# Loads cut into pieces of 256 to 320 KB, and SyncE waits before each transfer for the landing of the one issued four places ahead

## Chip, cores, metric

The kernel runs on one core of one Trainium2 chip, which has eight cores. The metric is the device time of one execution in microseconds (us). Before the change it is 707.77 us, the median of 3 runs (707.77 to 709.53).

## What is computed

One block of a network over 2048 positions with 640 channels, float32 throughout. A small vector `c` gives six rows of modulation (`w_mod` is 640 x 3840). A long convolution along the positions, gated by `q`, is followed by a two-layer perceptron of width 1728 with a squared ReLU.

```python
mod = (_silu(c) @ w_mod).reshape(1, 6, 1, -1)          # sa, ca, ga, sb, cb, gb
h = _layernorm(x) * (1 + ca) + sa                       # x = A_q, 2048 x 640
# _A_ref: a causal convolution of k with 4 taps, times v, then per channel a
# convolution with ssm_k over all 2048 positions (by rfft of length 4096),
# plus kv * ssm_D, times its first argument
x = x + ga * _A_ref(h, A_k, A_v, A_shift_k, A_ssm_k, A_ssm_D)
h = _layernorm(x) * (1 + cb) + sb
r = relu(h @ w1 + b1)
x = x + gb * ((r * r) @ w2 + b2)                        # w1 640 x 1728, w2 1728 x 640
```

## The kernel before

**Stages.** The channels are worked in five blocks b = 0 to 4 of 128. For each block K and V are loaded (`kv_load`, four quarters of 512 positions), transposed on TensorE (`kv_k`, `kv_v`), convolved and multiplied on VectorE (`kv_s`, `kv_m`), and stored to a scratch tensor `kv_d` in HBM in the same quarters (`kv_m`, 256 KB each). `load_x` reads them back in another layout: 128 partitions, each with 32 groups of 64 numbers, 1 MB a block. `load_h` reads the filter `ssm_k` in that layout, also 1 MB. The convolution is a Fourier transform made of matmuls. Its first step is `unit_a` (line 368, tile `pa`), which takes a quarter of a block at a time from the filter (i = 1) or from the data (i = 0). Then come `spectrum` (line 383, tiles `eh`, `h` and `x`; constants `gb`), the complex product on VectorE and GpSimd (`front`), the inverse steps `back` (line 449, tile `qp`, constants `gi`) and `unit_t`, `unit_y` (lines 513, 524). `skip` adds `ssm_D` to the filter; for b above 0 VectorE does it.

**Beside it.** The layer norm of `q` loads all of `q` in tiles of one to four rows of 128 positions (`q_big`, `q_ut`, both through `q_load`) and takes statistics on VectorE (`stats1`, line 284). For each block `q` is loaded again as a column strip of 1 MB (`load_xp`), scaled on ScalarE (`prep_a`) and gated. The sum goes to a second scratch tensor, `x1_d` (`finish_add`). The modulation rows come from `w_mod` in slabs of 320 KB (`part_load`), scaled on ScalarE (line 326) and added on GpSimd.

**The perceptron** starts at about 305 us: eight chunks of 256 positions, in each 14 steps over the width (lines 707 and 777). Its weights are loaded in slabs of 320 KB (`w_load`) into four staging buffers and split in two parts.

**Order.** The program is written as one list. A table (`at`, with the places `FS` and `GS`) puts each load and each piece of side work at a place among the TensorE steps, and `keep_order` at the end ties every engine to the order in which the program was written. Almost all transfers go through `sp_dma` (line 138), that is from SyncE (SP), which issues them one after the other: a transfer whose data or buffer isn't ready keeps all later ones waiting. A few small constants and two last pieces of the result are issued from ScalarE, two single rows from GpSimd.

**Sizes before.** `load_x(0)` and `load_x(1)` are cut into four pieces of 256 KB, the other `load_x` and all `load_h` after block 0 are single transfers of 1 MB (block 0's filter is loaded in four pieces by `load_h0`). `load_xp` is 1 MB, `q_load` 320 to 1280 KB, `load_gb` and `load_gi` 512 KB, four of each. Everything else is 320 KB or less, except `load_x1` with 640 KB in the perceptron.

**The one wait placed by hand** is `HOLD`: after `load_x(0)` and after `load_x(1)` the next transfer waits until the third of the four pieces has landed.

Of the kernel before, what the change touches and what calls it, by code (L numbers as in the profile page):

```python
# [18 lines left out]
P = 128  # L19
NB = D // P  # L20
NL = S // P
# [4 lines left out]
NC = S // CH  # L26
EPS = 1e-5
MLAG = 3
HOLD = {0: 2, 1: 2}


def _constants():
# [60 lines left out]
def ssm_mlp_kernel(  # L93
# [20 lines left out]
    nc = tc.nc  # L114
# [16 lines left out]
    kv_d = dr.tile([D, S], F32, tag="kv_d", name="kv_d")  # L131
    x1_d = dr.tile([S, D], F32, tag="x1_d", name="x1_d")

    behind = []


    def sp_dma(o, i):
        sp.dma_start(o, i)
        if behind:
            info = mybir.DependencyInfo(mybir.DependencyClass.Sync, mybir.DependencyReason.DATA)  # L140
            tc.add_manual_dep(nc.cur_bb.bb.instructions[-1], behind.pop(), info, reason="place in time")

    def copy(eng, o, i):
        if eng is act:
# [55 lines left out]
    def p_tile(b):  # L200
        pt[b] = sb.tile([P, 2, DG, 64], F32, tag=f"S{b % 2}", name=f"p_{b}")

    def load_h(b, n=1):
        w = DG // n
        for i in range(n):
            sp_dma(
                pt[b][:, 1, i * w : (i + 1) * w],
                hsrc[:, b * DG + i * w : b * DG + (i + 1) * w, :],
            )

    def load_x(b, n=1):
        w = DG // n
        for i in range(n):
            sp_dma(
                pt[b][:, 0, i * w : (i + 1) * w],
                xsrc[:, b * DG + i * w : b * DG + (i + 1) * w, :],
            )
            if i == HOLD.get(b):
                held = nc.cur_bb.bb.instructions[-1].name
        if b in HOLD:  # L220
            behind.append(held)


    def kv_load(i):
        b, h = divmod(i, 4)
        rows = slice(h * 512, (h + 1) * 512)
        cols = slice(b * P, (b + 1) * P)
        t = KN[h % (4 if b == 0 else 2)]
        for w, src in ((0, k), (1, v)):
            sp_dma(t[:, w], src[rows, cols].rearrange("(t p) d -> p t d", p=P))  # L230
# [128 lines left out]
    def unit_a(b, i, q):  # L359
        t = [  # L360
            ps.tile([P, 8, 32, 2], F32, tag="X", name=f"pa_{b}_{i}_{q}_{e}", bufs=4)
            for e in range(2)
        ]
        for g in range(8):
            for e in range(2):
                l = slice(64 * e, 64 * e + 64)
                for r in range(2):
                    pe.matmul(  # L368
                        t[e][64 * r : 64 * r + 64, g].rearrange("p m d -> p (m d)"),
                        pt[b][l, i, 8 * q + g, :],  # L370
                        cw[l, r],
                        start=True,
                        stop=True,
                    )
        for e in range(2):
            c = 64 * e + 16 * q
            o = AX[b][i][:, :, c : c + 16].rearrange("p m (g d) -> p m g d", d=2)
            copy(act, o, t[e].rearrange("p g m d -> p m g d"))
# [90 lines left out]

    def load_xp(b):  # L470
        t = sb.tile([P, NL, P], F32, tag=f"XP{b % 2}", name=f"xp_{b}")
        sp_dma(t, q[:, b * P : (b + 1) * P].rearrange("(l p) d -> p l d", p=P))
        XPt[b] = t

    def u_tile(b):
# [356 lines left out]
    def kv_all(h):  # L832
        kv_k(0, h)
        kv_s(0, h)
        kv_v(0, h, "T")
        kv_m(0, h)
# [11 lines left out]
    kv_all(2)  # L848
    unit_a(0, 1, 2)
    kv_all(3)  # L850
    load_x(0, 4)
    unit_a(0, 1, 3)
    load_gb(3)
    kv_load(4)
    load_gi(0)
    kv_load(5)
    load_gi(1)
    load_h(1)
    load_gi(2)
    load_gi(3)  # L860
# [10 lines left out]
    def FS(b, j):  # L871
        return 28 * b + j

    def GS(b, s):
        return 28 * b + 10 + s

    def at(i, fn, *args):
        tab[i].append((fn, args))
# [17 lines left out]
    for j in range(2):  # L896
# [5 lines left out]
        [GS(0, i) for i in (0, 1, 1, 2)],  # L902
        [GS(0, i) for i in (3, 4, 4, 5)],
    ], "TTYX")
    at(GS(0, 6), load_x, 1, 4)
    at(FS(1, 8), load_x, 2)
    at(GS(1, 16), load_x, 3)
    at(GS(2, 16), load_x, 4)
    at(FS(0, 2), p_tile, 2)
    at(GS(0, 14), load_h, 2)  # L910
    put_kv(2, [
        [GS(0, i) for i in (8, 9, 10, 11)],
# [4 lines left out]
    for b in (3, 4):  # L917
        at(GS(b - 2, 0), p_tile, b)
        put_kv(b, [[GS(b - 2, 4 * h + i) for i in range(4)] for h in range(4)])
        at(FS(2, 0) if b == 3 else GS(2, 1), load_h, b)  # L920


    def q_big(tag, l0):
        n = 4 if tag.startswith("XP") else 3 if tag == "UP1" else 2
        t = sb.tile([P, n, D], F32, tag=tag, name=f"q_{l0}", bufs=2 if tag == "X1" else None)
        q_load(t, l0, n)

    def q_load(t, l0, n):
        sp_dma(t, q[l0 * P : (l0 + n) * P, :].rearrange("(l p) d -> p l d", p=P))
        for i in range(n):  # L930
            qt[l0 + i] = t[:, i]

    def q_ut():
        q_load(UT.rearrange("p l d -> p (l d)")[:, 0:D].rearrange("p (l d) -> p l d", l=1), 15, 1)
# [8 lines left out]
    each(q_do, stats1, [(l,) for l in range(NL)])  # L943
    at(GS(1, 15), stats1_end)
    at(FS(1, 8), load_xp, 0)
    at(FS(2, 1), load_xp, 1)


# [45 lines left out]
    put4(finish_add, 0, [GS(2, s) for s in (3, 4, 5)], (1, 2, 3))  # L994
    put4(finish_stats, 0, [GS(2, s) for s in (5, 6, 7)], (1, 2, 3))
    at(GS(2, 8), load_xp, 2)
    put_u(1, [GS(2, s) for s in (5, 8, 11, 14)])
    put4(gate, 1, [FS(3, s) for s in (0, 1, 2, 3)])
# [221 lines left out]
    for i in range(len(seq) + MLAG):  # L1220
        if i >= MLAG:
            n, f = seq[i - MLAG]
# [7 lines left out]
        if i <= last:  # L1230
            n, f = seq[i]
# [42 lines left out]
```

## Time and profile before

| | |
|---|---|
| median of 3 runs | 707.77 us (707.77 to 709.53) |
| the profiled execution, its own time | 712.27 us |
| its span, first to last instruction | 710.5 us |
| mean granted TensorE clock | 0.989 |
| TensorE (matmul) busy | 666.4 us, 94% |
| VectorE, ScalarE, GpSimd busy | 47%, 47%, 42% |
| DMA: read from HBM, written | 58.98 MB, 14.42 MB |

How to read it: times are microseconds from the first instruction unless marked ns. PE is TensorE's matmuls and PEld its weight loads, which overlap; DVE is VectorE, ACT ScalarE, POOL GpSimd, SP SyncE. L368 is line 368 of the kernel. A "q" after an engine's name means its sequencer, which waits, branches and issues transfers. A row of the timeline reads: start, duration, engine, line, operation, output and inputs by the program's tile names, number of instructions merged, and in brackets the idle time before them with what ended it. "issue" there is time in which the engine waited for nothing that the profile shows. PEclk is the TensorE clock granted, as a share of full speed. In the DMA view q1 is SyncE's queue, q10 ScalarE's, and q8, of kind "instruction", carries packets of 16 KB; a row of issues gives KB each and the microseconds from issue to landing.

### The profile page before, as it was taken

The numbers are of one execution on the slowest core, as the hardware profiler recorded it, in microseconds if no ns is written. First come the engines' busy times: TensorE is split into PE (matmuls) and PEld (weight loads), VectorE is DVE, ScalarE is ACT, GpSimd is POOL, SyncE is SP. The second block draws the span as 40 slices with busy tenths as digits, with TensorE's granted clock in tenths as the row PEclk, the third lists the DMA queues.
The fourth block names the chain that finished last, engine by engine and source line by source line (L and its number), as shares of the span: only waits on it lengthen the run. The fifth ranks groups of instructions, "written<-read, shape, count | busy, mean of one in ns | idle before, by whom it ended". The sixth has DMA issues, their size and how long they took to land.

```text
span 710.5 us, 21027 instructions
## 1 busy us (share of the span) xinstructions
PE 666.4 (94%) x9164; PEld 636.5 (90%) x9164; DVE 336.3 (47%) x661; ACT 330.6 (47%) x685; POOL 295.1 (42%) x338
## 2 busy tenths in 40 slices
PE   6698889879899989999999999999999999999997
PEld 5687778769789879889999999999999999999996
DVE  5284745746877599669831222222313313312313
ACT  4535546666883886557533323323333333233221
POOL 1050036137845978942532522422514415325213
PEclk9999999999999999999999999999999999999999
DMA  9787795869465374328320020020020100200101
GB/s 251 211 248 253 213 259 169 240 192 256 107 186 138 91 195 151 88 88 238 98 75 1 1 75 1 1 75 2 10 66 1 39 37 1 75 1 1 39 1 38
DMA packets 88721, 74.76 MB, mean 105 GB/s; under 512 B 19250, under 2 KB 73906, under 8 KB 88628
## 3 DMA queue, kind: packets, MB, share of 16 engines
q1 hardware_dynamic: 86672, 72.86, 36.1%
q8 instruction: 72, 1.18, 0.7%
q10 hardware_dynamic: 1892, 0.54, 0.3%
q14 instruction: 21, 0.17, 0.1%
q0 software_dynamic: 64, 0.01, 0.0%
HBM read 58.98 MB, written 14.42 MB: 103 GB/s over the span
## 4 chain that ended last, share of the span: by engine, by line
PE 81%; DVE 8%; ACT 5%; issue 3%; DMA 2%; POOL 1%; DVEq 0%; POOLq 0%; SPq 0%; ACTq 0%
PE acc L777 26%; PE h L707 25%; PE qp L449 5%; PE x L383 4%; PE h L383 4%; PE y L524 4%; PE pa L368 4%; DVE KV L253 2%; PE t L513 2%; PE h L698 1%; PE xtp L672 1%; ACT a L145 1%; DVE kacc L253 1%; ACT q L145 1%; ACT KV L482 1%
## 5 line engine op out<-in xcount | busy, mean ns | idle before, releaser
L150 POOL TENSOR_TENSOR mtmp<-mtmp 128x256 f32<-128x256 f32 x112 | 72.1, 644 | 242.3 <-ACT mtmp L739 234.4
L707 PE MATMUL h<-xt,w_S 128*128 128x256 f32 x1290 | 167.0, 281 | 0.1
L707 PEld LDWEIGHTS h<-xt,w_S 128*128 128x128 f32 x1290 | 161.2, 190 | 0.4 <-DVE w_S L156 0.4
L777 PE MATMUL acc<-w_S,hring 128*128 128x320 f32 x960 | 156.8, 311 | 0.2 <-DVE hring L156 0.2
L156 DVE TENSOR_TENSOR hring<-mtmp,hring 128x256 fp32r<-128x256 f32 x112 | 64.9, 580 | 189.9 <-ACT hring L145 189.8
L777 PEld LDWEIGHTS acc<-w_S,hring 128*128 128x128 f32 x960 | 141.8, 188 | 0.7 <-DVE hring L156 0.7
L739 ACT ACTIVATE mtmp<-h,b1t 128x256 f32<-128x256 f32 x104 | 49.4, 475 | 177.6 <-PE h L707 172.2
L145 ACT ACTIVATE hring<-mtmp 128x256 fp32r<-128x256 f32 x112 | 46.7, 417 | 46.2 <-POOL mtmp L150 44.6
L368 PEld LDWEIGHTS pa<-wx,p 64*64 64x64 f32 x2560 | 44.7, 140 | 20.7 <-issue 12.1
L368 PE MATMUL pa<-wx,p 64*64 64x64 f32 x2560 | 51.1, 228 | 12.6 <-issue 3.9
L145 ACT ACTIVATE a<-pa 128x512 f32<-128x512 f32 x80 | 43.5, 599 | 26.7 <-PE pa L368 26.3
L524 PE MATMUL y<-wx,wx 128*64 128x64 f32 x1280 | 46.7, 227 | 8.5 <-ACT wx L145 5.5
L524 PEld LDWEIGHTS y<-wx,wx 128*64 128x64 f32 x1280 | 41.3, 139 | 13.3 <-ACT wx L145 6.2
L150 DVE TENSOR_TENSOR wx<-x,wx 128x512 f32<-128x512 f32 x64 | 40.9, 681 | 25.2 <-PE x L383 15.8
L156 POOL TENSOR_TENSOR we<-wx 128x256 f32<-128x256 f32 x20 | 15.9, 795 | 77.8 <-DVE wx L150 75.6
L674 DVE TENSOR_SCALAR we<-xtp,cbs 128x256 f32<-128x256 f32 x35 | 19.0, 544 | 51.8 <-PE xtp L672 51.8
L153 POOL TENSOR_TENSOR wm<-wm,wm 128x640 f32<-128x640 f32 x20 | 31.8, 1589 | 28.3 <-ACT wm L326 28.1
L383 PE MATMUL x<-a,gb 128*64 128x128 f32 x640 | 41.9, 274 | 1.2 <-ACT a L145 1.1
L253 DVE SCALAR_TENSOR_TENSOR KV<-kt,tap,KV 128x511 f32<-128x511 f32 (+2 forms) x48 | 35.5, 739 | 15.3 <-ACT ktail L145 13.3
L145 ACT ACTIVATE q<-qp 128x512 f32<-128x512 f32 (+1 forms) x40 | 21.3, 584 | 38.5 <-PE qp L449 38.5
L383 PEld LDWEIGHTS x<-a,gb 128*64 128x64 f32 x640 | 36.2, 137 | 2.3 <-ACT a L145 1.3
L383 PE MATMUL h<-a,gb 128*64 128x128 f32 x512 | 35.0, 280 | 0.0
(140 smaller groups left out, 1031.2 us busy)
## 6 DMA issues: line engine op xcount, KB each, us to landing
wm<-in_w_mod_dram SPq DMA_DIRECT2D x25, 320.0 KB, 5.3
KV<-in_A_k_dram SPq DMA_DIRECT2D x20, 256.0 KB, 5.8
KV<-in_A_v_dram SPq DMA_DIRECT2D x20, 256.0 KB, 4.6
xp<-in_A_q_dram SPq DMA_DIRECT2D x5, 1024.0 KB, 9.2
out_dram<-x SPq DMA_DIRECT2D x14, 320.0 KB, 2.8
w1s<-in_B_w_dram SPq DMA_DIRECT2D x13, 320.0 KB, 3.9
w2s<-in_B_w_dram SPq DMA_DIRECT2D x13, 320.0 KB, 3.9
kv_d<-KV SPq DMA_DIRECT2D x16, 256.0 KB, 4.2
```

The costliest lines, as they stand in the source:

```text
L145: act.activation(o, i, AF.Copy)
L150: eng.tensor_mul(o, a, b)
L153: eng.tensor_add(o, a, b)
L156: eng.tensor_sub(o, a, b)
L253: dve.scalar_tensor_tensor(o, x, tap[:, b, t : t + 1], o, op0=ALU.mult, op1=ALU.add)
L368: pe.matmul(t[e][64 * r : 64 * r + 64, g].rearrange("p m d -> p (m d)"), pt[b][l, i, 8 * q + g, :], cw[l, r], start=True, stop=True,)
L383: pe.matmul(t[64 * a : 64 * a + 64, s + r], gb[:, g, r, a], AX[b][i][:, 2 * g + a], start=True, stop=True,)
L449: pe.matmul(t[a][:, u], gi[l, 4 * j + u, r], w[r][l, u % 2], start=(r == 0), stop=(r == 1),)
L524: pe.matmul(y[64 * h : 64 * h + 64, 4 * (g % 2) + i].rearrange("p c l d -> p (c l d)"), tss[g][:, i, 64 * r : 64 * r + 64], ca[:, r, h], s ...
L707: pe.matmul(hps[n, f][:m], WI[1, f][:, a, b], XT[n][:, x, b], start=(b == 0 and i == 0), stop=(b == NB - 1 and i == 2),)
L739: act.activation(r[:m], h[:m], AF.Relu, bias=b1t[:m, f : f + 1])
L777: pe.matmul(acc[2 * s + i], h[:, a, s * P : (s + 1) * P], w[:, y, i * 320 : (i + 1) * 320], start=(f == 0 and ti == 0), stop=(f == NF - 1 ...
```

## The change

`sp_dma` remembers the name of every transfer that it issues. From the fifth on, each is given a dependency on the one four places ahead of it (`OUT = 4`): SyncE waits for that one's landing before it issues. `HOLD` and its two waits are gone. `load_h` and `load_x` always issue four pieces of 256 KB, `load_xp` four of 256 KB, `q_load` one piece of 320 KB for each row of 128 positions. `load_gb`, `load_gi` (512 KB) and `load_x1` (640 KB) keep their sizes. No arithmetic and no order changes.

```diff
-HOLD = {0: 2, 1: 2}
+OUT = 4
...
-    behind = []
+    queued = []
 
     def sp_dma(o, i):
         sp.dma_start(o, i)
-        if behind:
+        queued.append(nc.cur_bb.bb.instructions[-1].name)
+        if len(queued) > OUT:
             info = mybir.DependencyInfo(mybir.DependencyClass.Sync, mybir.DependencyReason.DATA)
-            tc.add_manual_dep(nc.cur_bb.bb.instructions[-1], behind.pop(), info, reason="place in time")
+            tc.add_manual_dep(nc.cur_bb.bb.instructions[-1], queued[-1 - OUT], info, reason="place in time")
...
-    def load_h(b, n=1):
+    def load_h(b, n=4):
...
-    def load_x(b, n=1):
+    def load_x(b, n=4):
...
-            if i == HOLD.get(b):
-                held = nc.cur_bb.bb.instructions[-1].name
-        if b in HOLD:
-            behind.append(held)
...
     def load_xp(b):
...
-        sp_dma(t, q[:, b * P : (b + 1) * P].rearrange("(l p) d -> p l d", p=P))
+        src = q[:, b * P : (b + 1) * P].rearrange("(l p) d -> p l d", p=P)
+        for l in range(0, NL, 4):
+            sp_dma(t[:, l : l + 4], src[:, l : l + 4])
...
-    load_x(0, 4)
+    load_x(0)
...
-    at(GS(0, 6), load_x, 1, 4)
+    at(GS(0, 6), load_x, 1)
...
     def q_load(t, l0, n):
-        sp_dma(t, q[l0 * P : (l0 + n) * P, :].rearrange("(l p) d -> p l d", p=P))
         for i in range(n):
+            sp_dma(t[:, i], q[(l0 + i) * P : (l0 + i + 1) * P, :])
             qt[l0 + i] = t[:, i]
```

## The prediction, made before the changed kernel ran

> **What bounds the kernel now.** First the page, then busy time by stretch.
>
> ```profile
> span 710.5 us, 21027 instructions
> PE 666.4 (94%) x9164; PEld 636.5 (90%) x9164; DVE 336.3 (47%) x661; ACT 330.6 (47%) x685; POOL 295.1 (42%) x338
> PE 81%; DVE 8%; ACT 5%; issue 3%; DMA 2%; POOL 1%; DVEq 0%; POOLq 0%; SPq 0%; ACTq 0%
> ...
> 0.00:305.00 305.00, 266.49 (x6121) 238.64 (x6122) 200.31 (x400) 185.03 (x367) 149.79 (x162) 0.98 0.70 192
> 305.00:710.50 405.50, 399.91 (x3044) 397.88 (x3042) 136.03 (x262) 145.54 (x318) 145.28 (x176) 1.00 0.13 40
> ```
>
> After 305 us PE is busy 399.91 of 405.50 us and the DMA engines 13%: nothing to win there by transfers. Before 305 us PE stands idle 38.5 us and DMA is busy 70%. The rest of this text is about that front part. Of the chain that ended last, 16% (DVE 8, ACT 5, DMA 2, POOL 1) isn't PE's: 114 us, nearly all in the front, so there about 37% ends on others and 63% on PE, its issue time included.
>
> Next, the idle places of PE whose releaser is "issue", from the timeline:
>
> ```profile
> 32.43 0.75 PE L368 MATMUL pa<-wx,p 64*64 64x64 f32 x37 [0.84 <-issue]
> 56.73 0.59 PE L449 MATMUL qp<-wx,gi 64*128 64x128 f32 x3 [1.48 <-issue]
> 91.16 1.13 PE L368 MATMUL pa<-wx,p 64*64 64x64 f32 x33 [2.89 <-issue]
> 135.96 0.60 PE L241 MATMUL kt<-ident,KV 128*128 128x128 f32 x4 [1.81 <-issue]
> 251.14 0.80 PE L524 MATMUL y<-wx,wx 128*64 128x64 f32 x20 [1.66 <-issue]
> ```
>
> PE waits there for no tile. What it waits for, the table of DMA queues shows: q8, kind "instruction", 1.18 MB in 72 packets, so 16 KB each.
>
> ```profile
> q8 instruction: 72, 1.18, 0.7%
> ```
>
> I took the times at which they begin and counted PE's instructions between them (matmuls and weight loads, the third and fourth figure of a row):
>
> ```profile
> 379.78:396.41 16.63, 16.63 (x130) 16.63 (x129) 4.34 (x8) 6.92 (x15) 5.29 (x8) 1.00 0.01 1
> 80.52:83.90 3.38, 2.98 (x129) 2.47 (x130) 3.31 (x9) 1.73 (x5) 0.00 (x0) 1.00 0.78 156
> 80.52:88.72 8.20, 5.65 (x227) 4.64 (x226) 8.02 (x21) 3.91 (x9) 0.00 (x0) 1.00 0.87 245
> 215.52:222.40 6.88, 6.88 (x126) 6.71 (x124) 5.79 (x9) 2.00 (x4) 4.54 (x7) 1.00 0.95 224
> 215.52:224.95 9.43, 9.43 (x170) 9.14 (x168) 8.31 (x13) 3.68 (x7) 5.41 (x8) 1.00 0.93 245
> ```
>
> With DMA at 1% a packet follows the last after 259 instructions. That is PE's code, fetched block by block. After the packet at 80.52 the next was due, by that count, at 83.90; it began at 88.72, 4.8 us late and 453 instructions on, and PE stood still until 91.16. In the stretch 83.9 to 88.6 the queue table has the first row below and no q8; the second is from 88.7 to 88.8:
>
> ```profile
> q1 hardware_dynamic: 1205, 1.43, 92.9%
> ...
> q8 instruction: 1, 0.02, 58.8%
> ```
>
> So a code block waits while SyncE's queue moves 1.43 MB. The counter-example is in the last two rows above: due at about 222.5, begun at 224.95, so 2.4 us late. Then the queue held four transfers of 320 KB (the DMA view from 215.3 to 221.5), the depth that the change allows everywhere:
>
> ```profile
> wm<-in_w_mod_dram SPq DMA_DIRECT2D x4, 320.0 KB, 5.7
> ```
>
> How deep the queue is now:
>
> ```profile
> SPq L138 <- DMA tap<-in_A_shift_k_dram: 1.3, 1, 1.3
> ...
> 35.97 10.78 SPq L138 DMA_DIRECT2D gi<-in_gi_dram  x2
> 88.65 9.70 SPq L138 DMA_DIRECT2D KV<-in_A_k_dram  x1
> ```
>
> SP waits for `tap`, which ScalarE issued and none of SP's transfers needs; it is the ninth transfer that does so, so eight may be out today, of up to 1280 KB. Around 36 and 89 us SP even sat 10 us in an issue.
>
> Last, the clock:
>
> ```profile
> 57.00:59.90 2.90, 2.90 (x31) 2.90 (x31) 0.00 (x0) 0.00 (x0) 0.00 (x0) 0.50 1.11 369
> 89.00:91.00 2.00, 0.00 (x0) 0.00 (x0) 0.00 (x0) 0.00 (x0) 0.00 (x0) 0.92 1.01 345
> 91.20:94.00 2.80, 2.80 (x53) 2.68 (x54) 0.00 (x0) 1.08 (x2) 0.00 (x0) 0.50 1.09 322
> ...
> 56.73 3.58 PE qp L449 x24
> 40.77 1.99 PE qp L449 x32
> ```
>
> Two of the stalls are followed by half clock (0.50); the `qp` block behind the first took 3.58 us instead of 1.99.
>
> **The change part by part.**
>
> *More issues.* 46 more transfers (12 for `load_h`, 9 for `load_x`, 15 for `load_xp`, 10 for `q_load`), each a median of 0.416 us of SP:
>
> ```profile
> L138 SPq DMA_DIRECT2D wm<-in_w_mod_dram x25: 328/416/4481, 71.2 to 241.8; - x25
> ```
>
> 19 us in all, inside the stretches where SP now stands in an issue (10.78 and 9.70 us above) or waits for data. On the path: 0. Without that cover each would make the next load 0.42 us late.
>
> *The window.* Behind a waiting SP stand all later loads: K and V (PE's transposes wait for them), `gi` and `gb` (PE), filters (`skip` on DVE), slabs (ACT), and stores whose buffers are reused. Does it starve them?
>
> ```profile
> 24.16 3.21 DMA p<-kv_d
> 27.51 1.16 PE pa L368 x64
> 28.71 1.16 PE pa L368 x64
> ...
> wm<-in_w_mod_dram SPq DMA_DIRECT2D x1, 320.0 KB, 3.0
> ```
>
> Into idle rings a 256 KB piece lands in 3.21 us, a 320 KB slab in 3.0 (issued at 81.8). Pieces that PE is waiting for come 1.2 us apart (27.51, 28.71). Four pieces are 4.8 us of work against 3.2 to get the next one: the rings don't run dry, and each load lands when it does now, since it stands in one queue either way, only its issue comes later. I take 0. Bounds: 1 us of gain where a filter piece lands sooner, 3.7 of loss (worked out under the rivals).
>
> The Trainium skill, page "DMA: Bandwidth & Descriptors", section "Bandwidth", says the contrary of this change: batch transfers to 1 MiB or more; its section "Anatomy of one DMA — SWDGE (gpsimd) path" gives about 2.0 us fixed for each. By it the sum would gain 46 x 2.0 = 92 us of queue time (an estimate from that page). The trace disagrees for pieces in flight together: 1.2 us apart, fixed part included.
>
> *HOLD gone.* The constants behind `load_x(0)` now wait for its first piece, 27.4 instead of 29.80:
>
> ```profile
> 29.80 0.35 SPq L138 DMA_DIRECT2D gb<-in_gb_dram  x1
> ...
> 49.94 2.06 PE L449 MATMUL qp<-we,gi 64*128 64x128 f32 x32 [0.23 <-DMA gi<-in_gi_dram]
> ```
>
> Gain at most the 0.23 us that PE waits for `gi`; loss at most 2.4 (two pieces of `p` overtaken, 1.2 each), of which the code stall of 0.84 at 32.43 would hide its own length. They stand ahead in the same queue, so 0.
>
> *Code.* With four transfers out a fetch is 2.4 us late instead of 4.8: at 91.16 the stall shrinks by 2.4 to 0.5 us. At 56.73 I take all of 1.48, at 135.96 1.25 of 1.81 (half a microsecond before it PE was waiting for ScalarE in any case). At 251.14 a 1 MB strip alone is out, now and then: 0. At 32.43: 0. Sum 2.4 + 1.48 + 1.25 = 5.1, between 0 (packets wait as now) and 8.7 (all five rows in full).
>
> *Clock.* The idle times left before these places are 1.5 and 1.7 us:
>
> ```profile
> 54.08 1.16 PE L368 MATMUL pa<-wx,p 64*64 64x64 f32 x64 [1.50 <-DVE p L153]
> 87.70 0.57 PE L368 MATMUL pa<-wx,p 64*64 64x64 f32 x23 [1.70 <-DVE KV L270]
> ```
>
> The 1.81 us at 135.96 left the clock whole, so I take both half-clock stretches as gone: 3.58 - 1.99 = 1.6, and half of the 2.8 us from 91.2 = 1.4. Sum 3.0, between 0 and 3.0.
>
> *Together* 8.1 us of PE time in the front. What is late next is VectorE and ScalarE; with 63% of the chain on PE, 5.1 us arrive. Against the profiled execution's own 712.27 us (span 710.5) that is 707.2; the median of the runs shown is 4.5 us lower, so 707.77 - 5.1 = 702.7.
>
> **The rivals.**
>
> *Code doesn't wait for depth.* If a fetch is held up by traffic as such, shallower queues change nothing: 707.8, within 1.5. For it: `gb` and `gi` keep 512 KB, so around 30 to 50 us four transfers can still be 1.5 MB, as much as the 1.43 MB above; the wait then isn't what the change says it shortens. Against it: 4.8 late with deep queues, 2.4 with four slabs. The Trainium skill, same page, section "Queues, rings and completion order", has each DMA engine take turns between queues packet by packet; by that rule a fetch never waits for 1.43 MB of another queue, and this rival holds. The trace disagrees at 83.9 to 88.7.
>
> *More comes through.* If DVE and ACT merely follow PE, and all five stalls go: 8.7 + 3.0 = 11.7 off at most, 8 to 11.7: about 698.
>
> *Slower: four are too few.* Place: the bursts of 30 to 60 and 82 to 109 us.
>
> ```profile
> DMA packets 22154, 15.14 MB, mean 252 GB/s; under 512 B 10240, under 2 KB 19691, under 8 KB 22146
> ...
> KV<-in_A_v_dram SPq DMA_DIRECT2D x20, 256.0 KB, 4.6
> ```
>
> The first 60 us move 252 GB/s. If the 4.6 us median from issue to landing of a V quarter isn't queueing but the transfer's own, four out give 4 x 262 KB / 4.6 us = 228 GB/s, and 57 us of burst become 10.5% longer: 6 us, of which 63%, 3.8, reach the end; PE then idles at 56 and 91 us anyway, so those gains go, and the 1.25 at 136 x 0.63 = 0.8 stays: 710.8. It decides from 4.2 us per landing (4 x 262 / 252). For it: the median lies above that, and PE has only 0.23 us to spare for `gi`. Against it: 3.0 and 3.21 us into idle rings.
>
> **How the numbers follow.** Forecast 0.48, no change 0.19, more 0.10, slower 0.23. About 0.3%, 2.1 us, is what a measurement of this kernel can tell from no change. The forecast's own range is 699.5 to 705.6; with the slower case and part of the larger gain the range is 698 to 711. Faster: 0.48 + 0.10 = 0.58; the same 0.19; slower 0.23.
>
> **What would show it.** PE's "issue" rows at 56, 91 and 136 us gone or under 0.6; no 0.50 clock near 57 and 92 (those at other places stay); a q8 packet never more than about 3 us behind its 256 instructions; no SP issue of 10 us; `gi` and K, V landing within a microsecond of now, so that PE's waits for them don't grow. Wrong would be: "issue" rows as before; or new PE waits named DMA on `kt`, `qp` or `pa`; or the same stalls moved to other places by a code block that falls elsewhere.

## The result, and the profile after

The changed kernel takes 710.51 us, the median of 20 runs (707.17 to 714.6); the kernel before, in 20 runs beside them, 707.09 (699.75 to 710.23). The ratio is 1.0058 with a 95% interval of 1.004 to 1.0077: slower by 0.58%, about 4.1 us (the two medians stand 3.4 us apart). Executions more than 1.5% above the fastest of their kernel are left out of the ratios, and e15's profile, which is of one, is not read. The forecast was 702.7, faster. The time lies inside the range of 698 to 711, at its slow end, and the sign is wrong.

The profiled execution of the changed kernel took 708.91 us of its own time, 1.6 us less than its median; that of the kernel before took 712.27, more than any of the 20 runs just named. So the two spans (707.1 and 710.5) order the kernels the wrong way round, and no difference between these two profiles can be taken for the effect of the change. That is the first thing to read here.

The page of the changed kernel, and its busy time before and after 305 us:

```profile
span 707.1 us, 21101 instructions
PE 666.6 (94%) x9164; PEld 636.4 (90%) x9164; DVE 335.2 (47%) x661; ACT 330.4 (47%) x685; POOL 295.1 (42%) x338
PE 69%; DMA 14%; DVE 7%; ACT 4%; POOL 3%; issue 2%; SPq 0%; POOLq 0%; DVEq 0%; ACTq 0%
```

```profile
0.00:305.00 305.00, 270.15 (x6140) 241.13 (x6141) 202.00 (x406) 187.86 (x375) 150.29 (x162) 0.98 0.72 192
305.00:707.10 402.10, 396.47 (x3026) 395.25 (x3024) 133.21 (x256) 142.58 (x312) 144.84 (x176) 1.00 0.12 40
```

PE's busy time is the same to 0.2 us, and the part behind 305 us still has PE busy but for 5.6 us. In the chain that ended last DMA has gone from 2% to 14% and PE's share from 81% to 69%: many links of the chain that PE's own work ended now end on a transfer. In two later profiles of the unchanged kernel (e1 and e13 below) DMA has 5% and 6%, so 14% is more than these three profiles of one kernel differ by.

Rows of PE's timeline at the places of the forecast:

```profile
34.83 0.85 PE L365 MATMUL pa<-wx,p 64*64 64x64 f32 x42 [1.66 <-issue]
...
56.41 1.16 PE L365 MATMUL pa<-wx,p 64*64 64x64 f32 x64 [1.81 <-DVE p L154]
...
86.95 1.18 PE L365 MATMUL pa<-wx,p 64*64 64x64 f32 x60 [1.73 <-DVE KV L267]
...
131.79 0.60 PE L238 MATMUL kt<-ident,KV 128*128 128x128 f32 x4 [1.97 <-ACT wx L146]
...
137.15 0.93 PE L365 MATMUL pa<-wx,p 64*64 64x64 f32 x48 [0.41 <-issue]
...
147.71 1.97 PE L523 MATMUL y<-wx,wx 128*64 128x64 f32 x32 [3.05 <-ACT wx L146]
```

The "issue" rows of 1.48 at 56.73, 2.89 at 91.16 and 1.81 at 135.96 have no successor over 0.41 us. The one near 32 us is there still, and twice as long (1.66 for 0.84). Near 132 PE now waits for ScalarE. The wait for ScalarE near 147 is not new: the kernel before has 3.72 us of it at 152.00, and e1 has this:

```profile
144.25 1.35 PE L524 MATMUL y<-wx,wx 128*64 128x64 f32 x32 [2.75 <-ACT wx L145]
```

Two of its stretches at half clock, from its busy time by stretch (the last three figures are granted clock, DMA share, GB/s):

```profile
28.00:31.00 3.00, 3.00 (x116) 3.00 (x120) 0.00 (x0) 1.09 (x2) 0.00 (x0) 0.50 1.28 241
...
148.00:153.00 5.00, 5.00 (x46) 3.63 (x44) 1.41 (x4) 2.49 (x4) 2.33 (x2) 0.50 0.66 187
```

There is no half clock near 57 and 92, but there is one at 28 and a long one at 148. These two need not be the change's doing: the unchanged kernel has half clock near 29 and 145 in e1 and near 28 and 147 in e13. Counted as in the prediction, by 259 instructions from packet to packet, no code packet between 20 and 300 us is more than 2.7 us late (4.8 in the first profile).

What SyncE issues, and how long landings take:

```profile
27.77 1.11 SPq L138 DMA_DIRECT2D gb<-in_gb_dram  x1
...
37.03 4.65 SPq L138 DMA_DIRECT2D p<-in_A_ssm_k_dram  x4
```

```profile
wm<-in_w_mod_dram SPq DMA_DIRECT2D x25, 320.0 KB, 4.3
KV<-in_A_k_dram SPq DMA_DIRECT2D x20, 256.0 KB, 4.1
KV<-in_A_v_dram SPq DMA_DIRECT2D x20, 256.0 KB, 4.1
...
gi<-in_gi_dram SPq DMA_DIRECT2D x4, 512.0 KB, 5.1
```

`gb` goes out at 27.77, 2 us earlier than the hold let it. The issues of 10 us are gone. K lands 4.1 us after its issue (5.8 before), V 4.1 (4.6), `gi` 5.1 (12.1): less queueing behind an issue, as the depth was cut; whether the data are there earlier doesn't follow from it.

### The profile page after: what moved, and what is told of

The parts are those of the page before. It is cut to its first block, busy times and chain, and to the rows that moved or that the text cites. A ratio compares the mean times of both kernels' runs of the same rounds, so it can differ in the third digit from the quotient of the medians.

```text
span 707.1 us, 21101 instructions
## 1 busy us (share of the span) xinstructions
PE 666.6 (94%) x9164; PEld 636.4 (90%) x9164; DVE 335.2 (47%) x661; ACT 330.4 (47%) x685; POOL 295.1 (42%) x338
## 4 chain that ended last, share of the span: by engine, by line
PE 69%; DMA 14%; DVE 7%; ACT 4%; POOL 3%; issue 2%; SPq 0%; POOLq 0%; DVEq 0%; ACTq 0%
PE acc L776 27%; PE h L706 25%; DMA KV<-in_A_k_dram 3%; PE qp L446 3%; PE h L380 2%; PE y L523 2%; DMA kv_d<-KV 2%; PE x L380 2%; DMA wm<-in_w_mod_dram 2%; DVE KV L250 2%; DMA p<-in_A_ssm_k_dram 2%; DMA p<-kv_d 2%; PE h L697 1%; DMA q<-in_A_q_dram 1%; PE pa L365 1%
```

## The experiments

Four theories for the loss. **One execution**: the stalls that were priced belonged to the execution profiled before, so there was little to win. **Pieces**: the cut transfers cost. **Start**: without the hold, `gb` and what follows get ahead of a code fetch near 30 us. **Window**: the waits for the fourth transfer back cost. All ratios are to the kernel before, timed on the same chip, with a 95% interval.

| kernel | hold | window of four | ratio | interval |
|---|---|---|---|---|
| e1, e13: unchanged | yes | no | 1.0027, 0.9988 | 0.9995 to 1.006, 0.9962 to 1.0014 |
| e2: pieces | yes | no | 0.9996 | 0.9965 to 1.0027 |
| e4 | none | no | 1.006 | 1.0025 to 1.0094 |
| e6 | x(0) only | no | 1.0017 | 0.9989 to 1.0045 |
| e7 | x(1) only | no | 1.0103 | 1.0059 to 1.0146 |
| e3 | none | all | 1.0059 | 1.0031 to 1.0087 |
| changed kernel | none | all, pieces | 1.0058 | 1.004 to 1.0077 |
| e9 | yes | all | 1.0059 | 1.003 to 1.0087 |
| e5 | yes | all, pieces | 1.0047 | 1.0021 to 1.0073 |
| e11, e16 | yes | first 40, pieces | 1.0047, 1.0049 | 1.0012 to 1.0081, 1.0018 to 1.008 |
| e10 | yes | from the 41st, pieces | 1.0067 | 1.0041 to 1.0093 |
| e17 | yes | 41 to 91, pieces | 1.0033 | 1.0004 to 1.0062 |
| e14 | yes | 92 to 126, pieces | 1.0011 | 0.9989 to 1.0033 |
| e18 | yes | from the 127th, pieces | 1.001 | 0.9988 to 1.0032 |
| e15 | yes | all but 92 to 126, pieces | 1.0043 | 1.0018 to 1.0069 |
| e8 | x(0), x(1), fourth piece | no | 1.0032 | 1.0 to 1.0064 |
| e12 | x(0), x(1), x(2) | no | 1.0014 | 0.9982 to 1.0045 |

### The kernel before, profiled again (e1, e13)

No edit.

> The kernel before, unchanged, for a second profile. Theory 'one execution' (the stalls that the prediction priced belonged to the execution that was profiled, at 712.27, and not to the kernel's usual run): the own time lies near 707, the instruction fetches behind the stalls at 91.16, 56.73 and 135.96 come less than half as late, and the half-clock stretches at 56.55 and 90.69 are gone or elsewhere, so there were under 2 us to win. Rival 'usual stalls': the same three stalls are there again with 4 us or more in all, and the loss lies in something the change added, of some 8 us. Ratio 1.000 in both.

> The kernel before once more, unchanged: how far from 1.000 a kernel comes out that differs in nothing. The first one gave 1.0027; 0.998 to 1.003 expected. If it comes out near 1.003 again, the ratios of all runs stand some 0.2 per cent too high; near 1.000, they can be taken as they are.

Medians 706.31 and 705.14 us; the two ratios lie on both sides of 1, so the other ratios can be taken as they are, each for what its interval allows. The spans are 706.2 and 705.4. In every profile read here, changed or not, the time from the perceptron's first matmul to the end is 401.3 to 401.7 us: whatever differs, differs before it. PE's timeline of e13 at the places of the forecast:

```profile
55.84 1.16 PE L368 MATMUL pa<-wx,p 64*64 64x64 f32 x64 [1.81 <-DVE p L153]
56.93 2.06 PE L449 MATMUL qp<-wx,gi 64*128 64x128 f32 x32
...
91.20 0.66 PE L241 MATMUL kt<-ident,KV 128*128 128x128 f32 x4 [1.40 <-DMA KV<-in_A_k_dram]
...
131.11 0.66 PE L241 MATMUL kt<-ident,KV 128*128 128x128 f32 x4
```

The `qp` block runs at full clock behind the first row, at 91 PE waits for K and not for code, and the `kt` transposes of the stage that stalled at 135.96 begin without any stall. In e1 the three "issue" rows are absent too. The first profile had 8.68 us in five "issue" rows; e1 has one of 0.73, at a new place, 200.47, and e13 none over 0.7. "One execution" holds as far as three profiles can tell: two of them have nothing of what was to be won. In e1, half-clock stretches lie at other places (29, 145, 186, 203, 254 us); they come and go between executions of one kernel.

### The pieces alone (e2)

```diff
-    def load_h(b, n=1):
+    def load_h(b, n=4):
...
-    def load_x(b, n=1):
+    def load_x(b, n=4):
...
-        sp_dma(t, q[:, b * P : (b + 1) * P].rearrange("(l p) d -> p l d", p=P))
+        src = q[:, b * P : (b + 1) * P].rearrange("(l p) d -> p l d", p=P)
+        for l in range(0, NL, 4):
+            sp_dma(t[:, l : l + 4], src[:, l : l + 4])
...
-        sp_dma(t, q[l0 * P : (l0 + n) * P, :].rearrange("(l p) d -> p l d", p=P))
         for i in range(n):
+            sp_dma(t[:, i], q[(l0 + i) * P : (l0 + i + 1) * P, :])
```

> Only the pieces: h, x, xp and q are cut as in the change; the hold of x(0) and x(1) is kept and there is no wait for the landing four places ahead. Theory 'pieces' (the smaller packets and 46 more issues cost the 4 us): 1.004 to 1.008. Rivals 'window' and 'start': 0.998 to 1.002.

0.9996: the 46 more issues and the smaller pieces cost nothing that can be measured. "Pieces" falls. In its profile the third stall is there again:

```profile
130.84 0.60 PE L241 MATMUL kt<-ident,KV 128*128 128x128 f32 x4 [1.69 <-issue]
```

So the stall isn't the large transfers' either: here it came with pieces, and in e13 it stayed away with whole ones.

### The hold alone (e4, e6, e7)

```diff
-HOLD = {0: 2, 1: 2}
+HOLD = {}          # e4
+HOLD = {0: 2}      # e6
+HOLD = {1: 2}      # e7
```

> Only the hold of x(0) and x(1) taken away; sizes as before, no window. Theory 'start': 1.003 to 1.006, first front of x near 36.8. Rivals 'window' and 'pieces': 0.998 to 1.002, first front of x near 34.4.

> The kernel before with the hold at x(0) alone. Theory 'start': 0.998 to 1.002. Rival 'second hold' (the transfers behind x(1) near 81 cost as much as those near 27): 1.003 to 1.005.

> The kernel before with the hold at x(1) alone. Theory 'start': 1.004 to 1.007, as without any hold, with pa stalled for 1.7 near 33 by the third code fetch. Rival 'second hold': 0.999 to 1.002.

With the hold of x(0) the kernel stays as it was (1.0017), without it it is slower (1.006 and 1.0103). The hold of x(1) makes no difference that these intervals can tell. PE's timeline of e1 first, with the hold:

```profile
27.45 1.16 PE L368 MATMUL pa<-wx,p 64*64 64x64 f32 x64 [2.42 <-DMA p<-kv_d]
28.84 4.77 PE L368 MATMUL pa<-wx,p 64*64 64x64 f32 x192 [0.23 <-DMA p<-kv_d]
34.74 1.09 PE L383 MATMUL x<-a,gb 128*64 128x128 f32 x16 [1.14 <-ACT a L145]
...
38.97 1.97 PE L383 MATMUL x<-a,gb 128*64 128x128 f32 x32
```

and of e4, without:

```profile
27.26 1.16 PE L368 MATMUL pa<-wx,p 64*64 64x64 f32 x64 [2.15 <-DMA p<-kv_d]
29.21 3.99 PE L368 MATMUL pa<-wx,p 64*64 64x64 f32 x150 [0.79 <-DMA p<-kv_d]
34.94 0.85 PE L368 MATMUL pa<-wx,p 64*64 64x64 f32 x42 [1.74 <-issue]
36.93 1.98 PE L383 MATMUL x<-a,gb 128*64 128x128 f32 x16 [1.14 <-ACT a L145]
...
42.56 1.97 PE L383 MATMUL x<-a,gb 128*64 128x128 f32 x32
```

Both begin the products of the data within 0.2 us of each other. Without the hold the second piece of `p` comes later (0.79 for 0.23), then the `pa` products break off with 42 to go and PE stands for 1.74 us with "issue"; the first `x` block starts 36.93 - 34.74 = 2.2 us later. It then runs at half clock (1.98 us for the 16 that took 1.09), and the third is 42.56 - 38.97 = 3.6 us late. In e7 the same row carries more:

```profile
34.84 0.85 PE L368 MATMUL pa<-wx,p 64*64 64x64 f32 x42 [3.48 <-issue]
```

The DMA view of 29 to 32 us shows what the hold does. With the hold (e1); the row DMA is the busy share of the engines in 40 equal slices:

```profile
DMA  9999999999999920000000000899525997925194
...
q1 hardware_dynamic: 886, 0.45, 73.4%
q8 instruction: 1, 0.02, 2.6%
```

Without it (e4):

```profile
DMA  9999999999995999561689598999897999899999
...
q1 hardware_dynamic: 1151, 0.85, 106.8%
```

SP's wait for the third piece lets SyncE's queue run dry, and from about 30.1 it moves nothing for some 0.8 us; the code packet begins as it drains, at 30.02. Without the wait there is no hole, 0.85 MB go by, and no code packet begins in the whole window; it comes at 32.37, too late for the last 42 `pa` matmuls. The changed kernel reads like e4 here: a first `x` block at 36.82, behind the 1.66 us at 34.83.

The other profiles say the same. In the fifteen with the hold of x(0) (the kernel before among them) this packet begins between 29.6 and 31.2 us, at most 0.8 us late by the prediction's count, and the stall before the last 42 `pa` matmuls is 1.2 us at most. In the four without it (e3, e4, e7, the changed kernel) the packet begins between 32.2 and 32.6, 2.0 to 3.0 us late, and the stall is 1.7 to 3.5 us. "Start" holds for the packet and the stall. How late the `x` block comes also depends on the clock: in e13, with the hold and no stall, but 6.83 us at half clock from 27.6, it begins at 36.24.

### The window, without and with the hold (e3, e9, e5)

```diff
 def sp_dma(o, i):
     sp.dma_start(o, i)
+    queued.append(nc.cur_bb.bb.instructions[-1].name)
+    if len(queued) > OUT:
+        info = mybir.DependencyInfo(mybir.DependencyClass.Sync, mybir.DependencyReason.DATA)
+        tc.add_manual_dep(nc.cur_bb.bb.instructions[-1], queued[-1 - OUT], info, reason="place in time")
```

e3 has this and no hold, e9 this and the hold, both with the sizes of before; e5 is the changed kernel with the hold of before put back.

> Only the window: each SyncE transfer waits for the landing of the one four places ahead, with the sizes of before, no hold. Theory 'window' (the waits make kv_d, KV and wm land late): 1.005 or more, with kv_d and wm named as what ACT waits for. Theory 'pieces': 0.998 to 1.002. Theory 'start' (without the hold, gb and what follows go out at 27.77 instead of 29.80 and the third code fetch comes 1.6 us later): 1.003 to 1.006, with the first front of x near 36.8 instead of 34.4.

> The changed kernel with the hold put back: the transfer behind x(0) and the one behind x(1) wait for the landing of the third piece of x, beside the wait for the one four places ahead; the sizes of the change. Theory 'start' (the loss is the hold's alone): 0.997 to 1.002, gb issued near 29.8 and the first front of x near 34. Rival 'window adds its own loss' (kv_d, wm and KV landing late for ACT): 1.003 to 1.006.

> The kernel before with the window of four added and the hold kept; sizes of before. Theory 'either costs the same' (the window delays the start by about as much as the missing hold does, and the two do not add up): 1.003 to 1.006. Rival 'only the hold matters' (the 1.0047 of the changed kernel with the hold was chance): 0.999 to 1.002.

Putting the hold back should have put the time back. It didn't: 1.0047 and 1.0059. In e5 the packet is on time (31.21), and PE has no "issue" row over 0.6 us before 200 us. The window costs about half a per cent of its own, so "start" alone is not the answer. Without the hold it costs nothing more: e3 and the changed kernel come out at 1.006 like e4, which has no window. Lost and lost does not add here, and the profiles suggest why: e4 has, beside the row at 34.94, "issue" rows of 2.08 us at 91.12 and at 137.03, and the changed kernel has neither. That the window takes these stalls away, as the forecast wanted, is likely but not shown, since the unchanged kernel loses them by itself in two profiles of three. The nineteen profiles read here lean that way. Take "issue" rows over 0.6 us at 86 to 92 and at 119 to 138 us. Where the window covers the transfers of that stretch, one of twelve cases has such a row (0.66 us); where it doesn't, 13 of 26 do. But all five kernels with the window over both stretches (e3, e5, e9, e10, the changed kernel) have one of 0.6 to 1.9 us near 198 to 208, where five of the other fourteen do.

At the start the limit does not help: e3, with the window and no hold, has the late packet as well, at 32.55, and this row:

```profile
35.42 0.85 PE L365 MATMUL pa<-wx,p 64*64 64x64 f32 x42 [2.58 <-issue]
```

### Which part of the window (e10, e11, e14 to e18)

Each is the changed kernel with the hold put back, and the dependency given only to some of SyncE's 243 transfers.

```diff
-        if len(queued) > OUT:
+        if len(queued) > 40:                                # e10
+        if OUT < len(queued) <= 40:                         # e11, e16
+        if 91 < len(queued) <= 126:                         # e14
+        if len(queued) > OUT and not 91 < len(queued) <= 126:   # e15
+        if 40 < len(queued) <= 91:                          # e17
+        if len(queued) > 126:                               # e18
```

> The changed kernel with the hold put back and the window only from SyncE's 41st transfer on, that is from about 50 us. If the window's loss lies in its waits at the start (gb and kv_d before x(0)): 0.999 to 1.002. If it lies in the later waits, where ACT waits for kv_d and wm near 91, 103, 130 and 146: 1.003 to 1.005.

> The changed kernel with the hold put back and the window only for SyncE's first 40 transfers, to about 50 us. The other way round: 1.003 to 1.005 if the window's loss lies at the start, with x(0) issued 0.5 to 1 us later than 24.18; 0.999 to 1.002 if it lies in the later waits.

> The changed kernel with the hold put back and the window for SyncE's transfers 92 to 126 alone (x(2), xp and the wm, KV and kv_d behind them, some 113 to 157 us). Theory 'the burst of x(2) and xp' (behind it wm, KV and kv_d go out later, and ACT waits for them until the y matmuls near 145): 1.003 to 1.006. Theory 'spread' (the window costs a little at every burst): 1.000 to 1.003.

> The changed kernel with the hold put back and the window everywhere but for SyncE's transfers 92 to 126. Theory 'the burst of x(2) and xp': 0.999 to 1.002, with ACT's waits for wm near 130 and 146 back at under 2 us in sum. Theory 'spread': 1.003 to 1.005.

> The window for the first 40 transfers with the hold and the pieces, once more, since its profile showed at most 0.8 us of loss to 45 us while its time came out at 1.0047. If that was chance: 0.999 to 1.002. If the window at the start costs what the first run said: 1.004 to 1.006, and the loss must then lie behind 45 us, in stalls of the kind seen at 56.26 and 87.67.

> The changed kernel with the hold put back and the window for SyncE's transfers 41 to 91 alone (some 50 to 113 us: q, KV, kv_d, x(1), h(2)). The window from the 41st on gave 1.0067, that for 92 to 126 alone 1.0011. If the late part of the loss lies at the burst of x(1) and h(2), where the profiles of window kernels show ACT waiting for kv_d near 92 and 104: 1.003 to 1.006. If it lies behind 157 us or needs both: 0.999 to 1.002.

> The changed kernel with the hold put back and the window from SyncE's 127th transfer on alone (some 157 us to the end). If the late part of the loss lies at x(1) and h(2): 0.999 to 1.002. If it lies behind 157 us, in the last SSM blocks and the loads of the weights: 1.003 to 1.006, with the delay to the kernel before growing between 160 and 290 us.

e10 and e11 were meant to decide between early and late; both lost, e10 more than either of its ranges allowed. The first 40 transfers cost 0.48%, measured twice; 41 to 91 cost 0.33%; 92 to 126 and the rest 0.1% each, no different from nothing. My guess that the burst of x(2) and xp carries it (e14, e15) was wrong; it is the two earlier bursts, to 113 us. The four parts sum to 1.0%, with an interval of about 0.5 either way by the intervals of the rows, against 0.47 and 0.59 for the whole: more than the whole, but within what these runs leave open.

How the window costs there is not shown. One candidate is that ScalarE waits longer for transfers. ACT's waits between 82 and 160 us in e13 first, then in the changed kernel, then in e10:

```profile
ACT wm L326 <- DMA wm<-in_w_mod_dram: 2.5, 2, 1.5
...
ACT KV L242 <- DMA kv_d<-KV: 0.7, 1, 0.7
```

```profile
ACT KV L239 <- DMA kv_d<-KV: 5.8, 3, 2.3
...
ACT wm L323 <- DMA wm<-in_w_mod_dram: 4.8, 2, 3.0
```

```profile
ACT KV L248 <- DMA kv_d<-KV: 7.1, 3, 2.5
...
ACT wm L332 <- DMA wm<-in_w_mod_dram: 6.2, 2, 4.2
```

That is 10.6 and 13.3 us in all, against 3.2. But e1, unchanged, has 8.0 and e12, without any window, 8.6, while e9, with the window everywhere, has 6.4: the ranges overlap, and one profile of a kernel does not carry it. A late landing can reach PE directly: in e10 the `kt` transposes wait for K itself, 2.91 us (e13, unchanged, has 1.40 of the same kind at 91.20).

```profile
132.37 0.60 PE L247 MATMUL kt<-ident,KV 128*128 128x128 f32 x4 [2.91 <-DMA KV<-in_A_k_dram]
```

For the first 40 transfers the profiles show no wait of that kind, and at most 0.6 us of delay to e1 by 45 us. What e11 and e16 both have is stalls without a named wait further on, where no window stands. In e11:

```profile
89.39 0.80 PE L374 MATMUL pa<-wx,p 64*64 64x64 f32 x36 [1.73 <-issue]
...
134.89 0.60 PE L247 MATMUL kt<-ident,KV 128*128 128x128 f32 x4 [1.41 <-issue]
```

and in e16:

```profile
88.34 0.81 PE L374 MATMUL pa<-wx,p 64*64 64x64 f32 x36 [1.19 <-issue]
...
134.06 0.60 PE L247 MATMUL kt<-ident,KV 128*128 128x128 f32 x4 [1.41 <-issue]
```

Those are the stalls of the first profile of the kernel before, in both profiles of this kernel and in one of three of the unchanged one. That a shift of half a microsecond at the start makes them likelier is a guess and stays open.

### More holds (e8, e12)

```diff
-HOLD = {0: 2, 1: 2}
+HOLD = {0: 3, 1: 3}          # e8
+HOLD = {0: 2, 1: 2, 2: 2}    # e12, with load_x(2) in four pieces
```

> The kernel before with both holds on the fourth and last piece of x instead of the third: gb goes out near 31 and not 29.9. Theory 'start', if the code fetch is what the hold protects: the third fetch comes no later than before, so 0.997 to 1.001. Rival 'what waits behind the hold is late too' (gb, KV, gi one place later): 1.002 to 1.004.

> The kernel before with a third hold of the same kind: x(2) in four pieces, and the xp transfer behind it waits for the third. If a hold behind each load keeps the code fetch on time: the stall of some 2 us with no releaser near 129 to 134 goes, 0.995 to 0.999. If what is held back (xp, then KV and wm) is needed at once: 1.000 to 1.004, with ACT or PE waiting for KV or wm near 130.

Neither wins: 1.0032 and 1.0014. In e8 the code packet near 30 is on time (30.01) and the kernel is none the faster; its rival, that what waits behind the hold is late too, had 1.002 to 1.004. In e12's profile the stalls near 119 and 130 are gone and its span is 702.7 us, but its median, 705.79, is that of the kernel before. No kernel here beats the one before.

## Why the prediction was wrong, point by point

Three steps failed. The gain (*Code* and *Clock*) was priced on stalls that the unchanged kernel need not have. *HOLD gone* was set to 0 and costs 0.6%. *The window* was set to 0 and costs 0.5%. The last two do not add, and why not stays open.

*More issues, 0 on the path.* Right: e2, with all 46 of them, 0.9996. The 92 us estimated beside that sum did not come; its 2.0 us stand under a heading on the gpsimd path, and these transfers go from SyncE.

*The window, 0, from 1 us of gain to 3.7 of loss.* Wrong in value: with the hold kept it costs 0.47% (e5) and 0.59% (e9), 3.3 to 4.2 us of 706, at the edge of its bound of loss. "The rings don't run dry, each load lands when it does now" was argued from one kind of piece, 1.2 us apart, in one burst; the stores of `kv_d` and the slabs of `wm` queued behind a waiting SP were named and then set to 0. Whether it is they that cost is not shown.

*HOLD gone, 0.* This is the step that failed outright: "They stand ahead in the same queue, so 0." The pieces of `p` do stand ahead; the code packet doesn't, it is in another queue. The same prediction had said that a code block waits while SyncE's queue moves its bytes, and did not apply it to the very wait that it saw removed. Its loss bound of 2.4 us was for overtaken pieces; measured is 2.2 us at the first `x` block and 3.6 at the third between the profiles of e1 and e4, and 0.6% of the time (e4). The code stall at 32.43 did not hide it: it grew, from 0.84 to 1.66 and 1.74.

*Code, 5.1 us, and Clock, 3.0.* The mechanism may be right in part: the three stalls and the two half-clock stretches are absent from the changed kernel's profile, and stalls near 90 and 130 us are rarer wherever the window stands. But the terms were priced on one execution, and the unchanged kernel need not have them: 8.68 us of "issue" rows in the first profile, 0.73 and 0 over 0.7 us in the next two. That four transfers out halve a fetch's delay is not borne out near 30 us: 2.0 and 2.1 us late with the window (e3, the changed kernel), 2.3 and 3.0 without it (e4, e7).

*Together.* The prediction noted that its profiled execution stood 4.5 us above the median, and then took the whole gain from the median. In that execution PE stood idle 44.1 us (its span less its busy time), against 38.1 and 39.1 in e1 and e13, with its busy time within 2 us of theirs: it was slow through its stalls, and they can't be taken away a second time from runs that haven't got them. Of the 5.1 us little was there to be had. (The lower end of its own range, 699.5, follows from no term either; 8.1 us in full give 699.7.)

*The rivals.* "Slower: four are too few" gave 710.8, and 710.5 came. That its time came out is in part luck. Half of it is right: the window costs, and the transfers whose window costs, the first 40 and 41 to 91, contain its bursts of 30 to 60 and 82 to 109 us. Its mechanism, too little bandwidth once a landing takes over 4.2 us, is not shown: K and V land in 4.1 us. In the two bursts the changed kernel moves 269 and 252 GB/s and e5 262 and 237, against 287 and 269 in e1 and 277 and 270 in e13; that is less, but not the 228 of the rival, and e4, without a window, has 258 and 266. And it did not contain the hold, whose absence makes the same loss without any window. "Code doesn't wait for depth" was given 0.19 and named no change, which did not come; but near 30 us its mechanism fits better than the forecast's. A queue of four delays the packet about as much as a deeper one there, and what lets it through on time is that the queue runs dry.

*What would show it.* "Issue" rows gone at three places: so it was, and it proved nothing, since they are gone in e1 and e13, the unchanged kernel, too. Half clock gone near 57 and 92: so it was, and gone in e1 and e13 as well. Code never more than about 3 us late: right between 20 and 300 us (2.7), but no more than 3.0 in e1 and e13 either. No SP issue of 10 us: right.

## What to carry to other kernels

A stall that is to be priced should be looked for in a second profile first, above all when the profiled execution is slower than the median: then its stalls may be what made it slow. A small hold that looks like an accident of order can be a gap by which a code fetch gets through; before removing a wait, ask what other queue uses the hole that it makes. A limit on transfers in flight is not free where almost every load and store shares one issuing engine: here it cost about 0.5%, and what stands behind the waiting transfer is issued later, whether it needed the limit or not.

## What the runs showed of the hardware

A code packet (q8) near 30 us came on time where SyncE's queue ran dry: in e1 the queue drained at about 30.1 and the packet began at 30.02; in e4, with the queue filled without a break, 0.85 MB went by between 29 and 32 us and it began at 32.37. Transfers limited to four in flight left no hole (the changed kernel, 32.20). A hole is not the only way in: the changed kernel's packet at 134.71 began while SyncE's queue took 77.7% of the engines' time (134.6 to 134.8 us).

One kernel's executions differ by more than this change: the unchanged kernel ran from 701.4 to 711.2 us beside e1, at a mean granted clock of 0.990, and the executions with the lower clock are the longer ones (a correlation of -0.77 over 30 runs). Each half-clock stretch in the traces, but for the one at the very end, is 3.41 us or twice that. The runs without a hold had a mean clock of 0.987 (nine of e4), but those of e1 and e2, which lose nothing that can be measured, had 0.988, so how much of the loss is clock stays open.
